# Linear attention, gated mixing and channel mixing on one core: the first block in float32 matmuls, the weights split in two only for the blocks behind it

## The chip, the cores and the metric

One core of a Trainium2 chip. The metric is the device time of one execution in microseconds (us). The engines are TensorE (PE; its weight loads are shown apart as PEld), VectorE (DVE), ScalarE (ACT), GpSimd (POOL) and SyncE (SP), which issues nearly all transfers.

## The reference

Three stages follow one another, all float32, with B=8, H=8, S=576, D=64, so 4608 rows of 512 values (weights and `conv_w` come as float64):

```python
q_s = softmax(q over d);  k_s = softmax(k over the sequence)
kv = einsum('bhsd,bhse->bhde', k_s, v);  x = einsum('bhsd,bhde->bhse', q_s, kv)   # x: 4608 x 512
gate = sigmoid(causal convolution of x, 5 taps, conv_w)
y = (gate * (x @ w_val)) @ w_out                                # 512x512 each
xk = mu_k*y + (1-mu_k)*y_prev;  xr = mu_r*y + (1-mu_r)*y_prev   # y_prev: one row earlier
out = sigmoid(xr @ w_r) * (relu(xk @ w_k)**2 @ w_v)             # 512x512, 512x1024, 1024x512
```

## The kernel before

The rows are cut into 12 blocks of T=384. Inside a block the 512 channels lie on partitions as 4 chunks of 128 and the 384 rows lie along the free axis. A block is a run of steps: V0 to V3 (x @ w_val, tile `pv`, one output chunk each), Y0 to Y3 (`py`), R0 to R3 (`racc`, one input chunk into three row tiles of 128x512), then H0 to H7 (`ph`) mixed with A0 to A7 (`vacc`, three row tiles, three steps behind H).

TensorE gets float32 accuracy from fp32r operands: each operand is a high part and a rest (`xh` and `xl`, `w_val_hi` and `w_val_lo`), and each product is three passes: high by high, high by rest, rest by high (L505 `products`, L559 for R, L591 for A, L448 for x). So a V, Y, H step is 12 passes of 384 columns for each output chunk, an R or A step 9 passes of 512.

Beside the steps stands the side work. Rounds (two for each batch, four heads each) make `kv`: `max` (DVE, tile `pm`), `turn` (transposes `pmT`, `mx`, exp of `kt`) and `mm` (`kvacc`). Then, for the next block, come `qload`, `qexp`, `qnorm` (softmax of q, tile `qt`), `xturn` (transposes `pq`), `x` (`px`) and `gate` (the convolution).

The weights arrive as 28 pieces of 128x512 float64 values, 512 KB each, in tiles `raw`. A piece is decoded to the negative of its float32 in place, by ACT (L148) and two DVE operations (L149, L150), and split at once: ACT writes the high part (L233), the rest comes from DVE (L235) for the names in `LOW_ON_VECTOR` and for the others from TensorE, an identity matmul of the decoded weight and one or two of the high part (tile `pl`, L241, L243) that ACT copies out (L244). Seven places hold such tiles: three in pool `first`, four in pool `early`.

In block 0 TensorE also computes the convolution of chunks 0, 2 and 3 (tile `pg`, L476, a diagonal matrix for each tap, built by ACT at L472), and ACT does the exp of q in 24 pieces of 128x64 (L385).

What stands where is written out by hand: `PROLOGUE` is all that comes ahead of V0, `FIRST` the side work behind each step of block 0, `REST` that of every later block. The building layer then places the instructions on the engines, and may move one past another there. An engine runs its instructions in order, and SP too: a load that waits for a place holds up those behind it. The order is the two queues' and the engines' own; there is no planner at run time.

Of the kernel before, what the change touches and what calls it, by code (L numbers as in the profile page):

```python
# [732 lines left out]
```

## Time and profile before

| | us |
|---|---|
| median of 3 runs (833.97, 835.52, 835.59) | 835.52 |
| the profiled execution | 834.17 |
| its span in the trace | 832.4 |
| TensorE busy in the span | 805.2 (97%) |
| VectorE busy | 565.8 (68%) |
| ScalarE busy | 505.6 (61%) |

The span starts with the first instruction that the trace shows, so the profiled execution is 1.77 us longer than its span. The first matmuls of V0 start at 47.09 us in block 0, at 127.90 in block 1 and at 192.90 in block 2. These three times cut the span into the stretches that the rows below use. A busy share is an average over the whole span: which engine ends a wait is read in each stretch.

### The profile page before, as it was taken

Reading aid. Unit: us, or ns where it says so; the run is one execution under the profiler, and the core shown is the slowest. Engines: PE = TensorE matmul, PEld = TensorE weight load, DVE = VectorE, ACT = ScalarE, POOL = GpSimd, SP = SyncE. Lnnn points to the kernel's source line nnn. Section 1 sums busy time; section 2 is a strip of 40 time slices with the busy share of each in tenths; the row PEclk is TensorE's granted clock in tenths of the full one; section 3 lists DMA queues with packets and bytes.
Section 4 is the critical chain, followed back from the end, with each engine's and each line's share of the span. In section 5 each row is a group of like instructions: output and inputs, shape, how many; then the busy total and the mean of one; then the engine's idle time right before and its main releaser. Section 6 shows DMA issues by size and latency. Waiting matters only on the chain.

```text
span 832.4 us, 12622 instructions
## 1 busy us (share of the span) xinstructions
PE 805.2 (97%) x4705; PEld 725.2 (87%) x4705; DVE 565.8 (68%) x1022; ACT 505.6 (61%) x1042; POOL 46.8 (6%) x208
## 2 busy tenths in 40 slices
PE   3699999999999999999999999999999999999998
PEld 2477888999989999999999999999998998998996
DVE  5799979677658578568576767757765866653621
ACT  5999674763763763763774674674674575564552
POOL 1001000100000100100000100100000000010000
PEclk9999999999999999999999999999999999999999
DMA  9688241211251211211232201202204101100101
GB/s 227 238 250 248 63 99 45 55 38 39 60 100 38 61 38 39 61 39 39 61 66 72 61 22 55 61 6 70 61 8 92 39 1 39 39 1 1 38 1 39
DMA packets 102124, 54.33 MB, mean 65 GB/s; under 512 B 85650, under 2 KB 93870, under 8 KB 102062
## 3 DMA queue, kind: packets, MB, share of 16 engines
q1 hardware_dynamic: 102016, 53.49, 24.9%
q8 instruction: 37, 0.61, 0.3%
q14 instruction: 25, 0.20, 0.1%
q10 hardware_dynamic: 46, 0.02, 0.0%
HBM read 44.06 MB, written 9.44 MB: 64 GB/s over the span
## 4 chain that ended last, share of the span: by engine, by line
PE 88%; DVE 4%; DMA 3%; ACT 2%; issue 1%; SPq 0%; DVEq 0%; ACTq 0%
PE vacc L591 23%; PE ph L505 23%; PE py L505 11%; PE pv L505 11%; PE racc L559 11%; PE px L448 3%; PE kvacc L327 3%; PE pq L433 2%; DMA raw<-in_moe_w_v_dram 1%; PE pg L476 1%; DMA raw<-in_moe_w_r_dram 1%; ACT qt L385 1%; DVE raw L150 1%; DMA raw<-in_moe_w_val_dram 1%; PE pl L241 1%
## 5 line engine op out<-in xcount | busy, mean ns | idle before, releaser
L505 PE MATMUL ph<-xkh,w_k_hi 128*128 128x384 f32 x384 | 132.5, 345 | 0.3 <-ACT yf L538 0.3
L505 PE MATMUL ph<-xkl,w_k_hi 128*128 128x384 f32 x384 | 129.2, 337 | 0.0
L505 PE MATMUL ph<-xkh,w_k_lo 128*128 128x384 f32 x384 | 129.1, 337 | 0.0
L406 DVE TENSOR_TENSOR kl<-rf,kh 128x384 fp32r<-128x384 f32 x96 | 53.4, 556 | 95.3 <-ACT kh L405 94.1
L591 PE MATMUL vacc<-w_v_hi,kl 128*128 128x512 f32 x288 | 112.7, 393 | 1.1 <-DVE kl L406 1.1
L591 PE MATMUL vacc<-w_v_hi,kh 128*128 128x512 f32 x288 | 113.4, 394 | 0.0
L591 PE MATMUL vacc<-w_v_lo,kh 128*128 128x512 f32 x288 | 112.7, 391 | 0.0
L495 DVE SCALAR_TENSOR_TENSOR gate<-xf,cw,gate 128x384 f32<-128x384 f32 x180 | 110.5, 616 | 2.9 <-ACT gate L493 0.2
L579 ACT ACTIVATE rf<-ph 128x384 f32<-128x384 f32 x96 | 47.0, 490 | 93.1 <-PE ph L505 92.6
L505 PEld LDWEIGHTS ph<-xkh,w_k_hi 128*128 128x128 f32 x384 | 72.2, 188 | 3.1 <-ACT yf L538 0.6
L548 DVE SCALAR_TENSOR_TENSOR xm<-yf,mus,xm 128x384 f32<-128x384 f32 x96 | 57.3, 616 | 25.6 <-ACT xm L547 25.1
L505 PEld LDWEIGHTS ph<-xkh,w_k_lo 128*128 128x128 f32 x384 | 72.4, 189 | 2.1
L505 PEld LDWEIGHTS ph<-xkl,w_k_hi 128*128 128x128 f32 x384 | 72.2, 188 | 0.4 <-DVE xkl L406 0.3
L591 PEld LDWEIGHTS vacc<-w_v_hi,kl 128*128 128x128 f32 x288 | 53.9, 188 | 13.1 <-DVE kl L406 1.7
L505 PE MATMUL pv<-xl,w_val_hi 128*128 128x384 f32 x192 | 65.1, 339 | 0.0
L505 PE MATMUL pv<-xh,w_val_hi 128*128 128x384 f32 x192 | 65.0, 338 | 0.0
L505 PE MATMUL py<-gh,w_out_hi 128*128 128x384 f32 x192 | 64.9, 345 | 0.0
L505 PE MATMUL pv<-xh,w_val_lo 128*128 128x384 f32 x192 | 64.8, 338 | 0.0
L505 PE MATMUL py<-gl,w_out_hi 128*128 128x384 f32 x192 | 63.3, 340 | 0.0
L505 PE MATMUL py<-gh,w_out_lo 128*128 128x384 f32 x192 | 63.1, 335 | 0.0
L591 PEld LDWEIGHTS vacc<-w_v_hi,kh 128*128 128x128 f32 x288 | 54.1, 188 | 8.9 <-ACT kh L405 0.3
L591 PEld LDWEIGHTS vacc<-w_v_lo,kh 128*128 128x128 f32 x288 | 54.1, 188 | 8.4
(132 smaller groups left out, 1665.9 us busy)
## 6 DMA issues: line engine op xcount, KB each, us to landing
out_dram<-rs SPq DMA_DIRECT2D x36, 256.0 KB, 2.0
kt<-in_k_dram SPq DMA_DIRECT2D x16, 512.0 KB, 4.7
vt<-in_v_dram SPq DMA_DIRECT2D x64, 128.0 KB, 3.8
qt<-in_q_dram SPq DMA_DIRECT2D x32, 256.0 KB, 4.2
raw<-in_moe_w_k_dram SPq DMA_DIRECT2D x8, 512.0 KB, 5.3
raw<-in_moe_w_v_dram SPq DMA_DIRECT2D x8, 512.0 KB, 4.4
kt<-in_k_dram SPq DMA_DIRECT2D x32, 64.0 KB, 4.2
raw<-in_moe_w_val_dram SPq DMA_DIRECT2D x4, 512.0 KB, 5.1
```

Source lines behind the costliest of these rows:

```text
L150: nc.vector.scalar_tensor_tensor(out=high, in0=high, scalar=3, in1=low, op0=ALU.logical_shift_left, op1=ALU.bitwise_or)
L241: nc.tensor.matmul(pl[:, 0:WC], lhsT=f32(ident), rhs=t, start=True, stop=False)
L327: nc.tensor.matmul(acc[e * D:(e + 1) * D, x * VW:(x + 1) * VW], lhsT=kt[:, 2 * x + e, s, :], rhs=st["v"][:, 2 * x + e, s, :], start=(s == ...
L406: nc.vector.tensor_sub(pair[1], a, f32(pair[0]))
L433: nc.tensor.transpose(pq[:, t * P:(t + 1) * P], qt[:, t, 2 * c:2 * c + 2, :].rearrange("p h d -> p (h d)"), f32(ident))
L448: nc.tensor.matmul(px[:, o:o + n], lhsT=kvs[b % 2][w][:, c, :], rhs=(qh, ql)[a][:, o:o + n], start=(m == 0), stop=(m == 2),)
L495: nc.vector.scalar_tensor_tensor(out=gx(gate), in0=xv[:, :, HALO - sh:HALO - sh + L], scalar=tap(c, HALO - sh), in1=gx(gate), op0=ALU.mult ...
L505: nc.tensor.matmul(po, lhsT=pairs_l[c][w], rhs=pairs_r[c][a], start=start and c == 0 and m == 0, stop=stop and c == n - 1 and m == 2,)
L548: nc.vector.scalar_tensor_tensor(out=gx(xf), in0=yv[:, :, 1:], scalar=mu[:, c:c + 1], in1=gx(xf), op0=ALU.mult, op1=ALU.add)
L559: nc.tensor.matmul(st["r"][t], lhsT=xr[a], rhs=W_r[w][:, c, :], start=(c == 0 and m == 0), stop=(c == NC - 1 and m == 2),)
L579: nc.scalar.activation(rf, ph[:, :T], AF.Relu)
L591: nc.tensor.matmul(st["v"][t], lhsT=kk[a], rhs=W_v[w][:, f, :], start=(f == 0 and m == 0), stop=(f == NF - 1 and m == 2),)
```

## The change

Block 0 is computed with plain float32 matmuls, one per product (the hardware takes two matmul instructions for it in the trace). Its operands are not split: `decode_weight` writes the float32 weight into a tile `whole`, without the sign change, and the splits (`swval0` and so on) are steps of their own, placed at the end of block 0 and in block 1, the high part on ACT, the rest (`lower`) on DVE for all 28. x of the blocks 0 and 1 is computed the same way from a float32 `kvf`. V and Y of block 0 go input chunk by input chunk into four PSUM banks (`row`), so V0 needs x chunk 0 and one weight piece only. No convolution is left on TensorE. q of block 0 comes with one transfer in packets of 768 bytes and v of the first two rounds in packets of 1 KB (tile `dense`, spread out by an ACT copy) where packets of 256 bytes were used, and the exp of q is one ACT instruction again, with DVE doing the subtraction. The raw tiles have six places on one side, which `dense` shares, and one place (pool `first`) for the seven pieces in `LEFT_WEIGHTS`. One list, `FRONT`, replaces `PROLOGUE` and `FIRST` and reaches over block 1. In block 1 and later the second and third pass of a product change places. `REST` stays for blocks 2 to 11.

```diff
-PROLOGUE = (
-    "lk0 lwval0 cload lv0 qload lwval1 lk1 lv1 lwval2 lwval3 lwout0 lwout1 lwout2 lwr0 lwr1 lwr2 lwr3 "
-    "lwk0 lwk1 lwk2 lwout3 lwk3 consts max0 wval0 turn0 mm0 max1 qexp wval1 turn1 mm1 qnorm wval2 xturn0 "
-    "x0 wval3 wout3 xturn1 x1 own0 xturn2 x2 xturn3 x3 wout0 wout1 wout2 own2 own1"
+FRONT = (
+    "lwout0 lk0 qload.0 lk1 max0 cload lv0 lv1 lwval0 lwval1 lwval2 lwval3 lwout1 lwr0 lwout2 lwout3 qexp.0 turn0 "
+    "lwr1 consts lwr2 vcopy0 wval3 qnorm.0 max1 mm0 vcopy1 turn1 xturn0.0 wval0 mm1 wval1 x0.0 wval2 lwr3 xturn1.0 "
+    "x1.0 gate0.0 xturn2.0 V0.0 gate1.0 xturn3.0 x2.0 V1.0 x3.0 V2.0 wout1 V3.0 gf0.0 wout0 gate3.0 gf1.0 gate2.0 "
+    "gf2.0 lwk0 lwk1 lwk2 lwk3 wout2 gf3.0 wout3 Y0.0 wr0 Y1.0 wr1 Y2.0 wr2 Y3.0 y0.0 wk1 y1.0 y2.0 y3.0 wr3 lwv1 "
+    "lwk4 mixk0.0 wk0 lwk5 lwk7 R0.0 R1.0 lwk6 mixk1.0 R2.0 mixk2.0 wk2 R3.0 mixk3.0 wk3 lwv3 lwv2 H0.0 lwv0 wv1 lwv4 "
+    "lwv5 H1.0 wv0 wk4 H2.0 wk5 rsig.0 A0.0 H3.0 wk6 A1.0 wk7 H4.0 wv2 max2 A2.0 H5.0 wv3 lwv6 lwv7 turn2 A3.0 H6.0 "
+    "mm2 max3 wv4 A4.0 wv7 wv6 H7.0 wv5 A5.0 turn3 qload.1 qexp.1 qnorm.1 xturn0.1 A6.0 swval3 x0.1 xturn1.1 x1.1 "
+    "swval0 A7.0 mm3 xturn2.1 gate0.1 x2.1 swval1 swval2 gate1.1 xturn3.1 x3.1 V0.1 gate2.1 V1.1 gate3.1 max4 V2.1 "
+    "turn4 swout1 swout0 V3.1 swout2 swout3 qload.2 kvsplit Y0.1 Y1.1 swr0 Y2.1 swr1 qexp.2 qnorm.2 swr2 Y3.1 swk1 "
+    "R0.1 mixk0.1 mixk1.1 R1.1 swr3 R2.1 mixk2.1 mixk3.1 swk0 R3.1 swk2 xturn0.2 swk3 swv1 H0.1 x0.2 xturn1.2 H1.1 "
+    "rsig.1 gate0.2 H2.1 swv0 swk4 swk5 A0.1 x1.2 xturn2.2 mm4 H3.1 swk6 swk7 A1.1 gate1.2 H4.1 swv2 x2.2 xturn3.2 "
+    "A2.1 swv3 H5.1 swv4 A3.1 H6.1 gate2.2 x3.2 swv7 swv6 A4.1 H7.1 swv5 A5.1 A6.1 A7.1 gate3.2"
 ).split()
-FIRST = {
-    1: "own3 wr1 wr0",
-    2: "wr2 wr3 wk0 wk1 wk2",
...
-    27: "gate3 gate2",
-}
...
+LEFT_GAP, RIGHT_GAP = 96, 224
-LOW_ON_VECTOR = "wval3 wout1 wout2 wout3 wr0 wr1 wr2 wk0 wk1 wk3 wk6 wk7 wv0 wv3 wv4 wv5 wv6 wv7".split()
-Q_ON_SCALAR = True
-CONV_ON_TENSOR = (0, 2, 3)
+CONV_ON_TENSOR = ()
-FIRST_WEIGHTS = "wval1 wval2 wval3 wout0 wout2 wr0 wr1 wr3 wk0 wk1 wk3".split()
+LEFT_WEIGHTS = "wval1 wout2 wr2 wr3 wk2 wk7 wv2".split()
...
-    def minus_float32(raw):
+    def decode(raw, out):
 
         low, high = raw[:, :, 0], raw[:, :, 1]
-        nc.scalar.activation(f32(high), f32(high), AF.Prelu, scale=-(2.0 ** -112), alpha=2.0 ** 32)
+        nc.scalar.activation(f32(high), f32(high), AF.Prelu, scale=2.0 ** -112, alpha=2.0 ** 32)
         nc.vector.tensor_scalar(out=low, in0=low, scalar1=29, scalar2=None, op0=ALU.logical_shift_right)
         nc.vector.scalar_tensor_tensor(
-            out=high, in0=high, scalar=3, in1=low, op0=ALU.logical_shift_left, op1=ALU.bitwise_or
+            out=out.bitcast(U32), in0=high, scalar=3, in1=low, op0=ALU.logical_shift_left, op1=ALU.bitwise_or
         )
-        return f32(high)
...
-        scale = 0.5 if pair is W_out or pair is W_v else 1.0
-        t = minus_float32(raws[name])
-        h, l = hi[:, kc, c0:c0 + WC], lo[:, kc, c0:c0 + WC]
-        nc.scalar.activation(h, t, AF.Copy, scale=-scale)
-        if name in LOW_ON_VECTOR:
-            nc.vector.scalar_tensor_tensor(
-                out=l, in0=t, scalar=-scale, in1=f32(h), op0=ALU.mult, op1=ALU.subtract
-            )
-        else:
-            pl = ps_acc.tile([P, 512], F32, tag="acc", name="pl")
-            n = int(1 / scale)
-            nc.tensor.matmul(pl[:, 0:WC], lhsT=f32(ident), rhs=t, start=True, stop=False)
-            for x in range(n):
-                nc.tensor.matmul(pl[:, 0:WC], lhsT=ident, rhs=h, start=False, stop=x == n - 1)
-            nc.scalar.activation(l, pl[:, 0:WC], AF.Copy, scale=-scale)
+    PLACES = len(CHUNKS) + 1
+    raws, whole, upper, lower = {}, {}, {}, {}
+
+    def place(dtype, name):
+        return wts.tile([P, WC], dtype, tag="w", bufs=PLACES, name=name)
+
+    def load_weight(n):
+        w, (kc, c0) = CHUNKS[n]
+        here = n in LEFT_WEIGHTS
+        raw = raws[n] = (first if here else early).tile([P, WC, 2], U32, tag="raw", bufs=1 if here else 6, name="raw")
+    def decode_weight(n):
+        w, at = CHUNKS[n]
+        whole[w, at] = place(F32, "whole")
+        decode(raws[n], whole[w, at])
...
+        h, t = upper[w][:, kc, c0:c0 + WC], whole[at]
+        l = lower[at] = place(F32R, "lower")
+        scale = 0.5 if w in HALF else 1.0
+        nc.scalar.activation(h, t, AF.Copy, scale=scale)
+        nc.vector.scalar_tensor_tensor(out=l, in0=t, scalar=scale, in1=f32(h), op0=ALU.mult, op1=ALU.subtract)
+
+    def weight(i, w, kc, c0, n):
+
+        at = w, (kc, c0 // WC * WC)
+        o = c0 % WC
+        if i == 0:
+            return (whole[at][:, o:o + n],)
+        return upper[w][:, kc, c0:c0 + n], lower[at][:, o:o + n]
...
+        if b == 0:
+            st["dense"] = early.tile([P, HR, NS4, D], F32, tag="raw", bufs=6, name="dense")
+            nc.sync.dma_start(
+                st["dense"].rearrange("p h s d -> p h (s d)"), src[:, 0:KT, :].rearrange("h (p s) d -> p h (s d)", s=NS4)
+            )
+    def v_copy(st):
+        nc.scalar.copy(st["v"][:, :, 0:NS4, 0:D], st["dense"])
...
+        if b < 2:
+            for e in range(2):
+                p = slice(e * D, (e + 1) * D)
+                nc.vector.tensor_mul(
+                    kvf[b][p, n * j:n * (j + 1), p], sums[p, :, 0:D], d3[p].to_broadcast([D, n, D])
+                )
+            return
...
+            came = first.tile([P, H, NT, D], F32, name="came")
+            nc.sync.dma_start(
+                came.rearrange("p h t d -> p h (t d)"), q[0, :, 0:T, :].rearrange("h (p t) d -> p h (t d)", t=NT)
+            )
+            return qt, came
...
-        for x in range(n):
-            nc.scalar.activation(a[:, x, :], a[:, x, :], AF.Exp, bias=qm[:, x:x + 1], accum_out=qs[:, x:x + 1])
...
-    PASSES = ((0, 0), (0, 1), (1, 0))
+    def passes(po, left, right, start, stop):
+
+        m = ((0, 0),) if len(left) == 1 else ((0, 0), (1, 0), (0, 1))
+        for x, (a, b) in enumerate(m):
+            nc.tensor.matmul(
+                po, lhsT=left[a], rhs=right[b], start=start and x == 0, stop=stop and x == len(m) - 1
+            )
...
+            kv = (kvf[b],) if i < 2 else kvs[b % 2]
+            passes(px[:, o:o + n], tuple(a[:, c, :] for a in kv), tuple(a[:, o:o + n] for a in st["q", c]), True, True)
...
+        def row(po, w, c, a):
+
+            for m in range(NC):
+                passes(po[m][:, :T], weight(i, w, c, m * P, P), a, c == 0, c == NC - 1)
...
+                row(st["pv"], "wval", m, xs["x", m])
+                row(st["py"], "wout", c, st["g", c])
...
+                passes(st["r"][t], part(st["xr", c], t), weight(i, "wr", c, 0, DM), c == 0, c == NC - 1)
...
+                    passes(st["v"][t], part(st["k", f], t), weight(i, "wv", f, 0, DM), f == 0, f == NF - 1)
```

SP, the first transfers, before (`kt`, `vt`, `qt` are k, v and q; `raw` a weight piece):

```order
L273 DMA kt<-in_k_dram 128x4x256
L278 DMA kt<-in_k_dram 64x4x64 x2
L221 DMA raw<-in_moe_w_val_dram 128x1024
L285 DMA vt<-in_v_dram 128x4x64 x4
L286 DMA vt<-in_v_dram 64x4x64
L362 DMA qt<-in_q_dram 128x8x64 x3
L221 DMA raw<-in_moe_w_val_dram 128x1024
L273 DMA kt_117<-in_k_dram 128x4x256
L278 DMA kt_117<-in_k_dram 64x4x64 x2
L285 DMA vt_118<-in_v_dram 128x4x64 x4
L286 DMA vt_118<-in_v_dram 64x4x64
L221 DMA raw<-in_moe_w_val_dram 128x1024 x2
```

and after:

```order
L205 DMA raw<-in_moe_w_out_dram 128x1024
L272 DMA kt<-in_k_dram 128x4x256
L277 DMA kt<-in_k_dram 64x4x64 x2
L382 DMA came<-in_q_dram 128x8x192
L272 DMA kt_115<-in_k_dram 128x4x256
L277 DMA kt_115<-in_k_dram 64x4x64 x2
L285 DMA dense<-in_v_dram 128x4x256
L291 DMA vt<-in_v_dram 64x4x64
L285 DMA dense<-in_v_dram 128x4x256
L291 DMA vt_116<-in_v_dram 64x4x64
L205 DMA raw<-in_moe_w_val_dram 128x1024 x4
L205 DMA raw<-in_moe_w_out_dram 128x1024
```

A piece of w_out comes first, the q of block 0 is one transfer instead of three, the v of a round is two instead of five, and all four pieces of w_val stand together behind them.

TensorE ahead of V0, before (`pq` are transposes of q, `px` makes x, `pg` the convolution, `pv` is V0):

```order
L433 MATMUL pq<-ident,qt 128x128 x3
L243 MATMUL pl<-w_out_hi,ident 128x512 x2
L448 MATMUL px<-qh,kv_hi_108 128x384
L448 MATMUL px<-qh,kv_lo_109 128x384
L476 MATMUL pg<-xf,diag 128x384
L448 MATMUL px<-ql,kv_hi_108 128x384
L476 MATMUL pg<-xf,diag 128x384 x4
L505 MATMUL pv<-xh,w_val_hi 128x384
```

and after:

```order
L335 MATMUL kvacc<-vt_116,kt_115 64x65 x20
L457 MATMUL pq<-ident,qt 128x128 x3
L430 MATMUL pv<-xf,whole 128x384
L430 MATMUL px<-q,kvf_108 128x384
L457 MATMUL pq<-ident,qt 128x128 x3
L430 MATMUL pv<-xf,whole 128x384 x3
L457 MATMUL pq<-ident,qt 128x128 x3
L430 MATMUL px<-q,kvf_108 128x384
```

V0 starts behind the first chunk of x instead of behind all four and the convolution, and the other chunks follow between its matmuls.

VectorE in block 1 around its Y and R steps, before (`gl`, `xrl`, `xkl` are rests of activations that PE waits for, `xm` the mixes, `pm` and `kt` a round, `qs` and `qt` q):

```order
L406 TENSOR_TENSOR gl<-gf,gh 128x384
L526 SCALAR_TENSOR_TENSOR gf<-gate,pv 128x384
L314 TENSOR_TENSOR kt<-kt,mx 128x1280
L406 TENSOR_TENSOR gl<-gf,gh 128x384
L393 TENSOR_REDUCE qs<-qt 128x24
L394 TENSOR_SCALAR qs<-qs 128x24
L548 SCALAR_TENSOR_TENSOR xm<-yf,mus,xm 128x384
L395 RECIPROCAL qs<-qs 128x24
L396 TENSOR_TENSOR qt<-qt,qs 128x1536
L406 TENSOR_TENSOR xrl<-xm,xrh 128x384
```

and after:

```order
L423 TENSOR_TENSOR gl<-gf,gh 128x384
L399 TENSOR_REDUCE qm<-qt 128x24
L322 TENSOR_TENSOR kt<-kt,mx 128x1280
L593 SCALAR_TENSOR_TENSOR xm<-yf,mus,xm 128x384 x2
L400 TENSOR_TENSOR qt<-qt,qm 128x1536
L423 TENSOR_TENSOR xrl<-xm,xrh 128x384
L593 SCALAR_TENSOR_TENSOR xm<-yf,mus,xm 128x384
L423 TENSOR_TENSOR xrl<-xm,xrh 128x384
L231 SCALAR_TENSOR_TENSOR lower<-whole,wk_hi 128x512 x2
L423 TENSOR_TENSOR xrl<-xm,xrh 128x384
L407 TENSOR_REDUCE qs<-qt 128x24
L593 SCALAR_TENSOR_TENSOR xm<-yf,mus,xm 128x384
```

Two weight splits (`lower`) stand between the `xrl` of R1 and R2 now, and the maximum, the subtraction and the sum of the next q (`qm`, `qt`, `qs`) stand in the same run, where only the sum and the division stood.

## Rows read from the trace of the kernel before

**Rows 1.** Windows: four stretches; busy us (instructions) per engine, clock, DMA share, GB/s.

```profile
0.00:47.09 47.09, 26.71 (x147) 16.45 (x148) 32.52 (x67) 36.85 (x111) 6.04 (x32) 1.00 0.84 233
47.09:127.90 80.81, 79.07 (x456) 65.90 (x455) 71.11 (x130) 63.21 (x124) 5.08 (x20) 1.00 0.55 154
127.90:192.90 65.00, 63.79 (x370) 58.31 (x369) 49.39 (x87) 39.18 (x77) 4.41 (x13) 1.00 0.18 45
192.90:832.40 639.50, 635.60 (x3737) 584.53 (x3735) 412.79 (x741) 366.40 (x732) 31.22 (x143) 1.00 0.18 44
```

**Rows 2.** Waits of PE, 47.09 to 832.4: us in total, times, longest.

```profile
PE pmT L301 <- DVE pm L294: 1.2, 1, 1.2
```

**Rows 3.** Chain that ended last, 0 to 60: start us, us, what.

```profile
2.99 4.86 DMA raw<-in_moe_w_val_dram
...
9.86 2.08 PE pl L241 x2
...
20.82 4.69 ACT qt L385 x28
...
33.69 6.23 DMA raw<-in_moe_w_r_dram
...
44.97 2.58 PE pg L476 x8
...
57.19 0.90 PE pl L241 x2
```

**Rows 4.** Windows by 10 us, columns as in rows 1.

```profile
0.00:10.00 10.00, 0.54 (x3) 0.44 (x3) 4.50 (x11) 3.94 (x11) 3.79 (x25) 1.00 0.77 193
10.00:20.00 10.00, 6.55 (x48) 4.21 (x49) 5.36 (x10) 7.01 (x22) 0.00 (x0) 1.00 1.24 255
20.00:30.00 10.00, 4.47 (x25) 1.87 (x25) 7.00 (x14) 9.78 (x45) 0.00 (x0) 1.00 0.50 175
30.00:40.00 10.00, 9.03 (x55) 6.00 (x52) 9.00 (x22) 9.08 (x21) 1.24 (x5) 1.00 0.86 290
```

**Rows 5.** Waits of SP's queue, 0 to 130: us in total, times, longest.

```profile
SPq L221 <- PE pl L241: 13.1, 6, 4.1
```

**Rows 6.** Chain, 700 to 795: three-pass products of a late block.

```profile
708.50 8.35 PE pv L505 x48
...
778.43 8.47 PE py L505 x48
786.90 8.20 PE racc L559 x36
```

**Rows 7.** Windows for tile pl alone, block 0: PE, PEld, ACT busy.

```profile
47.09:127.90 80.81, 8.58 (x20) 3.55 (x20) 3.59 (x6) 1.00 0.55 154
```

**Rows 8.** The same for tile pg.

```profile
47.09:127.90 80.81, 4.12 (x12) 1.79 (x10) 1.01 (x2) 1.00 0.55 154
```

**Rows 9.** Chain, 128 to 195: a round's matmuls and one chunk's q transposes.

```profile
142.61 1.32 PE kvacc L327 x40
...
158.57 0.33 PE pq L433 x3
```

**Rows 10.** VectorE groups, 47.09 to 127.9: busy us, mean ns, idle before.

```profile
L150 DVE SCALAR_TENSOR_TENSOR raw<-raw 128x512 uint32<-128x512 uint32 x17 | 11.7, 690 | 0.3 <-ACT raw L148 0.2
L495 DVE SCALAR_TENSOR_TENSOR gate<-xf,cw,gate 128x384 f32<-128x384 f32 x12 | 7.4, 617 | 0.5 <-ACT gate L493 0.2
L149 DVE TENSOR_SCALAR raw<-raw 128x512 uint32<-128x512 uint32 x16 | 6.7, 427 | 0.9 <-DMA raw<-in_moe_w_v_dram 0.9
...
L235 DVE SCALAR_TENSOR_TENSOR w_v_lo<-raw,w_v_hi 128x512 fp32r<-128x512 f32 x6 | 4.2, 693 | 0.3 <-ACT w_v_hi L233 0.2
L373 DVE TENSOR_TENSOR qt<-qt,qm 128x1536 f32<-128x1536 f32 x2 | 3.5, 1756 | 0.0
```

**Rows 11.** ScalarE groups, same stretch and columns.

```profile
L148 ACT ACTIVATE raw<-raw 128x512 f32<-128x512 f32 x17 | 11.5, 683 | 2.2 <-DMA raw<-in_moe_w_v_dram 1.7 <-DMA raw<-in_moe_w_k_dram 0.4
...
L233 ACT ACTIVATE w_v_hi<-raw 128x512 fp32r<-128x512 f32 x8 | 5.3, 667 | 0.0
```

More of the change, by code (lines that the diff above doesn't have):

```diff
@@ L188, in tap @@
         return cw[:, t * NC + c:t * NC + c + 1]
-    def gap(pool, size, name):
-        pool.tile([P, size // 4], F32, name=f"gap_{name}")
-    def weight(name, rows, cols, pool=wts):
-        hi = pool.tile([P, rows // P, cols], F32R, name=f"{name}_hi")
-        lo = pool.tile([P, rows // P, cols], F32R, name=f"{name}_lo")
-        return hi, lo
-    W_val = weight("w_val", DM, DM)
-    gap(wts, 64, "out")
-    W_out = weight("w_out", DM, DM)
-    gap(wts, 128, "k")
-    W_k = weight("w_k", DM, DFF)
@@ new lines, in tile_linear_attention_gated_conv_channel_mix @@
+    HALF = ("wout", "wv")
+    SHAPES = {"wval": (w_val, DM, DM), "wout": (w_out, DM, DM), "wr": (w_r, DM, DM), "wk": (w_k, DM, DFF), "wv": (w_v, DFF, DM)}
+    CHUNKS = {
+        f"{w}{x}": (w, at) for w, (_, rows, width) in SHAPES.items()
+        for x, at in enumerate((kc, c0) for c0 in range(0, width, WC) for kc in range(rows // P))
+    }
+    PLACES = len(CHUNKS) + 1
+    raws, whole, upper, lower = {}, {}, {}, {}
+    def place(dtype, name):
+        return wts.tile([P, WC], dtype, tag="w", bufs=PLACES, name=name)
@@ L499, in x_gate @@
         nc.scalar.activation(gate, gate, AF.Tanh, scale=0.5)
-    def products(po, pairs_l, pairs_r, start, stop):
-        n = len(pairs_l)
-        for c in range(n):
-            for m, (a, w) in enumerate(PASSES):
-                nc.tensor.matmul(
-                    po, lhsT=pairs_l[c][w], rhs=pairs_r[c][a],
-                    start=start and c == 0 and m == 0, stop=stop and c == n - 1 and m == 2,
-                )
-    def cols(pair, kc, c0, n):
-        return tuple(t[:, kc, c0:c0 + n] for t in pair)
     def main_steps(i, xs):
@@ L550, in mix, with part @@
             )
[L551 removed]
+            st[key, c] = (xf,) if i == 0 else split(xf, pair(key))
+        def part(pair, t):
+            return tuple(a[:, t * P:(t + 1) * P] for a in pair)
         def r(c):
             if c == 0:
[L555 removed]
+                st["r"] = [bank(ps_acc, "acc", f"racc{t}") for t in range(NT)]
             for t in range(NT):
[L557 to L562 removed]
+                passes(st["r"][t], part(st["xr", c], t), weight(i, "wr", c, 0, DM), c == 0, c == NC - 1)
         def rsig():
@@ L676, in tile_linear_attention_gated_conv_channel_mix @@
-    own = {f"own{c}": lambda c=c, st=xs: x_gate(st, 0, c) for c in range(NC)}
-    pro.update(own)
-    pro.update(weight_parts("wval", w_val, W_val, DM, DM))
-    pro.update(weight_parts("wout", w_out, W_out, DM, DM))
-    wide = weight_parts("wr", w_r, W_r, DM, DM)
-    wide.update(weight_parts("wk", w_k, W_k, DM, DFF))
-    wide.update(weight_parts("wv", w_v, W_v, DFF, DM))
-    pro.update(wide)
-    with tc.issue_after(cast.ins):
-        for n in PROLOGUE:
-            pro[n]()
-    for i in range(NB):
-        steps, side = main_steps(i, xs)
-        side.update(rounds_of(take_rounds((1, 1, 2)[i % 3] if i else NR)))
-        xs = {}
-        if i + 1 < NB:
-            side.update(attention(i + 1, xs))
-        if i == 0:
-            side.update(wide)
-            side.update(own)
-        for x, f in enumerate(steps):
+        todo_front[f"lk{x}"] = lambda x=x: k_load(rounds[x])
@@ L697, in tile_linear_attention_gated_conv_channel_mix @@
+    with tc.issue_after(cast.ins):
+        for n in FRONT:
+            todo_front.pop(n)()
+            if n == START:
+                break
+    for n in FRONT[FRONT.index(START) + 1:]:
+        todo_front.pop(n)()
+    for i in range(2, NB):
+        steps, side = main_steps(i, acts[i])
+        side.update(rounds_of(new_rounds(i)))
+        if i + 1 < NB:
+            side.update(attention(i + 1, acts[i + 1]))
+        for x, f in enumerate(steps.values()):
             f()
-            for n in (REST if i else FIRST).get(x, "").split():
+            for n in REST.get(x, "").split():
```

274 lines of the change are left out of this document (136 added, 138 removed).

## The prediction

> **What bounds the kernel now.** I read the windows by stage first [rows 1], then PE's waits, then the chain that ended last. From the first matmul of V0 on (47.09 us) PE is busy 79.07 of 80.81 us in block 0, 63.79 of 65.00 in block 1 and 635.60 of 639.50 in the ten blocks behind. Its longest wait there is 1.2 us, once [rows 2]. So from 47.09 on the time is PE's own work, and DVE (71.11 us in block 0) and ACT (63.21) run beside it. Ahead of 47.09 PE is busy 26.71 us only, and the chain there [rows 3] goes through loads of 4.86 and 6.23 us, a run of 4.69 us of the exp pieces on ACT, and 2.58 us of the convolution on PE. The transfers move 193, 255, 175 and 290 GB/s in the four stretches of 10 us [rows 4]. Time can therefore be won in two places: the 47 us ahead of V0, and PE's work in block 0. The ten late blocks keep their work.
>
> **Prices.** A fp32r pass of 384 columns is 8.35/48 = 0.174 us, one of 512 columns 8.20/36 = 0.228 [rows 6], so three passes are 0.522 and 0.683. A float32 product of 384 columns is two instructions; eight of the convolution's take 2.58 us [rows 3], so one product is 0.645. For 512 columns the nearest row is the identity matmul of a weight, 0.90 for the pair at 57.19 [rows 3], reading every second word; by columns of the convolution's row it would be 0.86. I take 0.88. A float32 product thus costs more than three passes here, 0.645 against 0.522: the change adds PE work where it replaces products, and must win by what it takes away and by starting earlier.
>
> The Trainium skill ("FP8 and Floating Point Precision", section "TensorE Precision Notes") says that true float32 takes four passes through the array. Four passes by the rows would be 0.696 and 0.911, and with them the sum below would be 4.4 us longer; the convolution's row shows less, and the row decides.
>
> **The change, part by part.**
>
> *Start of V0, 47.09 to 29.* V0 now needs one chunk of x and one piece of w_val. The exp of q becomes one instruction, the convolution's matmuls and diagonal matrices go, and no weight is split. Loads then end last. Ahead of V0 stand in SP's order: a piece of w_out 0.52 MB, k of two rounds 1.31, q 0.79, v of two rounds 1.18, four pieces of w_val 2.10. A second piece of w_out, 0.52, counts too, because DVE does its shift ahead of the last decode step of w_val and runs in order. Together 6.42 MB. The kernel before has moved 1.93 + 2.55 = 4.48 MB by 20 us [rows 4]; the other 1.94 at 255 to 290 GB/s end at 26.7 to 27.6. Behind them come one shift (0.43) and two decode steps of 0.69 [rows 10]: 28.5 to 29.4. I take 29, that is -18.1. The lower end, without the second w_out piece, is 27. The upper end, the 193 GB/s of the first stretch throughout, is 33.3 + 1.8 = 35.1.
>
> *Block 0 on PE, 80.8 to 85.4.* From V0 to the V0 of block 1:
> - V: 16 products at 0.645 = 10.3; three chunks of x behind its start 1.9 and two sets of q transposes at 0.33 [rows 9] 0.7: 12.9.
> - Two products at double price at the start, 1.3. In the trace a float32 pair took 2.08 at 9.86 us and 0.90 at 57.19 [rows 3], and V0 now lies between.
> - Y 10.3; R 12 at 0.88 = 10.6; H 32 at 0.645 = 20.6; A 24 at 0.88 = 21.1.
> - Two kv rounds: 1.32 [rows 9] and four transposes at 0.11, together 3.5; one wait of PE such as the row shows, 1.2 [rows 2].
> - x of block 1, four times 0.33 + 0.645 = 3.9.
>
> Together 85.4, which is +4.6. As a check: the products alone rise from 58.0 to 73.0, while the identity matmuls of the splits (8.58 [rows 7]) and the convolution (4.12 [rows 8]) leave the stretch, and three chunks of x come into it. DVE takes over the convolution of all chunks, 16 steps of 0.62 [rows 10] in block 0, ahead of Y; PE's V hides them, with some 2 us to spare by my count of DVE's row (11 gate steps, 4 decode steps and 3 shifts ahead of the first `gf`, 10.9 us, end it at 41 where Y0 starts at 43). Without that cover Y0 waits for the difference.
>
> *Block 1, 65.0 to 66.2.* The splits that stood in block 0 come here for w_k and w_v: 16 times 0.69 on DVE [rows 10] and 0.67 on ACT [rows 11]. With them DVE has 49.4 + 11.0 = 60.4 us in 65, ACT 49.9. So it fits, and PE's work hides it, but two splits stand directly ahead of the rest that R2 needs, and the subtraction of the next q (1.76 [rows 10]) in the same run. I charge 1.2, the size of the one wait in the trace [rows 2]; the ends are 0 and 4 (all of the run's splits and the subtraction late once).
>
> *Nothing for:* the other order of passes in blocks 1 to 11. The rows hold 0.174 for V and 8.47/48 = 0.176 for Y [rows 6]; that spread, 2 ns over some 1900 passes of a kind, is 4 us either way at most, and I take 0. The ACT copies of v, 2 pieces, lie beside loads. The first piece of w_out ahead of k costs 2 us of the start and is in the 6.42 MB.
>
> The sum against the profiled execution: 834.17 - 18.1 + 4.6 + 1.2 = 821.9. The median of the runs is 1.35 above that execution, so 823.
>
> **Rivals.**
>
> *Weights come late.* Seven pieces share one place: each is loaded (4.86 to 6.23 us [rows 3]), decoded (0.68 on ACT, 0.43 and 0.69 on DVE), and only then the next can start, and SP holds back all loads behind one that waits; six such waits took 13.1 us in the kernel before [rows 5]. Block 0 on PE is now the consumer from 29 us on. By my count H0 has some 3 us to spare on the fifth piece of that chain (w_k) and A0 about as much on its first w_v piece. If each of five steps takes 2 us more than the load and the decode alone, because the decode stands behind gates in DVE's row, PE waits 10 - 3 = 7 us: 830. A start by the upper end, 35.1, gives 829. For it: the serial chain and the queue order. Against: the loads behind it have six places, and moved 290 GB/s between 30 and 40.
>
> *Better start.* V0 at 27, no double price, no wait in block 1: 823 - 2 - 1.3 - 1.2 - 1.2 = 817.
>
> *TensorE stays at the price of the start, slower than before.* The early pair cost 2.08 where the later cost 0.90 [rows 3], and PE was busy 6.55 and 4.47 of 10 us from 10 to 30 [rows 4]; the granted clock column reads 1.00 in all stretches. If the matmuls of V, Y and R, 31.2 us, all ran at double price, the time would be 823 + 31 = 854. It decides from 12.5 us of float32 work at double price, some 19 products. Against it: PE has hardly a gap from V0 on, and the pair at 57.19, in a stretch without gaps, is at the low price.
>
> The Trainium skill ("TensorE: Matmul & The Clock Gate", "Part 1: The HAM clock gate") says that the array's clock is halved when the engine has been idle and comes back with work. By it V0 after the waiting of the start would begin at the low clock; the 2.08 against 0.90 agrees with that in size, while the clock column does not show it.
>
> *V0 does not move.* If a load that I have not counted holds x or w_val until 42 us or later, -5 of start against +4.6 + 1.2 leaves the time within 0.2%. Nothing in the rows asks for it: q, k and w_val are all issued ahead.
>
> **How the numbers follow.** The forecast, 818 to 828, has 0.63; late weights or start, 829 to 833, 0.18; the better start 0.09; the slow price 0.06; no movement 0.04. The first three are faster, together 0.90. The range of 815 to 832 holds the forecast, the better start for the most part and most of the late case, some 0.82. About 0.2% (1.7 us) is what a measurement of this kernel can tell from no change. Faster by more than that 0.90, within it 0.04, slower 0.06.
>
> **What would show it.** In the changed profile: the first `pv` at 29 (27 to 33 is right, above 35 the start was mis-sized); V, Y and H products 0.645 apart in the chain and R and A 0.86 to 0.90; the V0 of block 1 at 114 and of block 2 at 181; the ten late blocks 639.5 us within 2. Late weights would show as PE waiting on `whole` in R, H or A of block 0, and in the chain as loads into `raw`. The slow price would show as products 1.2 us and more apart with PE full. Block 1 over 69 us with PE waiting for `xrl` or `kl` would mean that the splits on DVE have become the bound there. The prediction is wrong if PE works with gaps between 29 and 114.

## The result

The changed kernel takes 825.15 us (median of 4 runs, 823.94 to 826.32), the kernel before 834.75 (4 runs, 833.85 to 835.59): a ratio of 0.9885, 95% interval 0.9864 to 0.9906, so 1.15% faster. The profiled execution took 824.69 us, its span 822.9, and the cuts by V0 give this table:

| stretch | before [rows 1] | predicted | after |
|---|---|---|---|
| up to V0 of block 0 | 47.09 | 29 | 27.21 |
| block 0 | 80.81 | 85.4 | 86.07 |
| block 1 | 65.00 | 66.2 | 66.91 |
| blocks 2 to 11 | 639.50 | 639.5 | 642.71 |
| span | 832.4 | 820.1 | 822.9 |

One sentence ahead of the prediction is too wide: the second and third pass of a product change places in R and A alone. V, Y, H and x keep their order.

The windows of the changed kernel, cut at its own V0 starts (the columns are those of [rows 1]):

```profile
0.00:27.21 27.21, 11.15 (x99) 7.74 (x99) 18.85 (x37) 12.70 (x19) 4.72 (x28) 1.00 0.85 287
27.21:113.28 86.07, 83.99 (x329) 46.50 (x329) 68.42 (x128) 51.52 (x96) 7.69 (x20) 1.00 0.55 169
113.28:180.19 66.91, 64.98 (x370) 58.63 (x370) 65.16 (x111) 50.52 (x102) 6.20 (x19) 1.00 0.25 59
180.19:822.90 642.71, 638.49 (x3737) 585.57 (x3735) 410.47 (x737) 365.88 (x731) 30.98 (x142) 1.00 0.16 44
```

TensorE is still busy nearly throughout. It starts its blocks 19.9 us earlier, pays 5.3 us more in block 0 and 1.9 more in block 1, and, what was not forecast, 3.2 more in the ten late blocks, whose work is the same. In block 1 VectorE is busy 65.16 of 66.91 us, where it was 49.39 of 65.00.

The chain that ended last up to V0 (start us, us, what):

```profile
3.07 5.76 DMA came<-in_q_dram
...
10.94 1.67 DVE qt L400
...
13.74 1.48 DVE kt L322
15.21 1.66 DVE qs L407
...
17.99 1.76 DVE qt L410
...
21.10 0.91 PE pq L457 x3
...
22.56 1.65 PE px L430 x2
24.21 2.37 PE kvacc L335 x40
26.58 0.83 PE pq L457 x3
27.41 1.00 PE pv L430 x2
28.41 0.65 PE px L430 x2
```

One transfer, that of q, then VectorE's work on q and k nearly without a gap from 10.9 to 20 us, then TensorE. No load of a weight stands in it. The last five rows show a price that falls: a product of 384 columns (`px`, two instructions) costs 1.65 us at 22.56 and 0.65 at 28.41.

What TensorE waited for from 27 to 113 us, and from 113 to 190 (us in total, times, longest):

```profile
PE racc L430 <- DVE xm L593: 1.0, 1, 1.0
PE px L430 <- ACT q L463: 0.6, 1, 0.6
PE kvacc L335 <- ACT kt L325: 0.5, 1, 0.5
```

```profile
PE py L430 <- DVE gf L566: 1.8, 1, 1.8
```

Three short waits in block 0, none of them for a weight by this view, and one of 1.8 us in the first Y step of block 1. The wait of 1.0 us, for a mix (`xm`), goes back to a weight all the same. In the chain that ended last, ahead of it:

```profile
42.27 7.42 DMA raw<-in_moe_w_k_dram
...
49.70 0.71 ACT raw L141
50.41 0.38 ACT yf L584
```

A piece of w_k lands, ACT decodes it, and only then comes the copy of y (`yf`) from which the mix is made.

### The profile page after: what moved, and what is told of

Same layout as the page of the kernel before. It is cut to its first block, busy times and chain, and to the rows that moved or that the text cites. A ratio compares the mean times of both kernels' runs of the same rounds, so it can differ in the third digit from the quotient of the medians.

```text
span 822.9 us, 12129 instructions
## 1 busy us (share of the span) xinstructions
PE 798.6 (97%) x4530; PEld 698.4 (85%) x4530; DVE 562.9 (68%) x1010; ACT 480.6 (58%) x947; POOL 49.6 (6%) x208
## 4 chain that ended last, share of the span: by engine, by line
PE 89%; DVE 5%; DMA 2%; ACT 2%; issue 1%; SPq 0%; DVEq 0%; ACTq 0%
PE vacc L430 24%; PE ph L430 23%; PE pv L430 11%; PE py L430 11%; PE racc L430 11%; PE px L430 4%; PE kvacc L335 3%; PE pq L457 2%; DVE whole L143 1%; DMA raw<-in_moe_w_k_dram 1%; DMA raw<-in_moe_w_v_dram 1%; DVE gate L525 1%; DMA came<-in_q_dram 1%; DVE xm L593 0%; DVE qt L400 0%
## 5 line engine op out<-in xcount | busy, mean ns | idle before, releaser
L430 PE MATMUL ph<-xkh,wk_hi 128*128 128x384 f32 x352 | 121.2, 344 | 0.0
L430 PE MATMUL ph<-xkl,wk_hi 128*128 128x384 f32 x352 | 118.7, 337 | 0.0
L430 PE MATMUL ph<-xkh,lower 128*128 128x384 f32 x352 | 118.3, 336 | 0.0
L430 PE MATMUL vacc<-lower,kh 128*128 128x512 f32 x264 | 104.1, 394 | 0.0
L430 PE MATMUL vacc<-wv_hi,kl 128*128 128x512 f32 x264 | 103.9, 394 | 0.0
L430 PE MATMUL vacc<-wv_hi,kh 128*128 128x512 f32 x264 | 103.8, 394 | 0.0
L430 PEld LDWEIGHTS ph<-xkh,wk_hi 128*128 128x128 f32 x352 | 66.2, 188 | 2.3
L430 PEld LDWEIGHTS ph<-xkh,lower 128*128 128x128 f32 x352 | 66.2, 188 | 2.0
L430 PEld LDWEIGHTS ph<-xkl,wk_hi 128*128 128x128 f32 x352 | 66.0, 188 | 0.0
L430 PE MATMUL py<-gh,wout_hi 128*128 128x384 f32 x176 | 59.8, 346 | 1.8 <-DVE gf L566 1.8
```

The source lines that it names most:

```text
L430: nc.tensor.matmul(po, lhsT=left[a], rhs=right[b], start=start and x == 0, stop=stop and x == len(m) - 1)
```

## Experiments

Experiments 1 to 11 are one run each, so they are read by their stages and waits and not by their total. Two stages differ from run to run even where nothing in them was changed: in the changed kernel and the seven runs with the same start and block 0 (e1, e2, e5, e8, e9, e11, e12), V0 comes between 26.8 and 28.2 us and block 0 takes 84.8 to 86.4.

### The late blocks: four runs on the pace

Rows of the late blocks, before (chain, start us, us, what):

```profile
735.93 2.08 PE ph L505 x12
...
745.95 2.06 PE vacc L591 x9
```

and after:

```profile
749.12 2.08 PE vacc L430 x9
751.21 2.10 PE ph L430 x12
...
776.87 8.20 PE racc L430 x36
```

One H step is 0.02 us longer and one A step too; R takes 8.20 for 36, as in [rows 6]. Eighty steps of each kind come to about 3 us, which is the difference. The table has the time of the chain's pieces over their matmuls, from the V0 of block 2 on (the expectations below have H and A of the changed kernel 0.1 lower):

| kernel | H, ns | A, ns | R, ns | late blocks, us |
|---|---|---|---|---|
| before | 174.5 | 229.4 | 227.8 | 639.5 |
| changed | 175.9 | 231.2 | 227.8 | 642.7 |
| e1_shift | 175.6 | 232.9 | 227.9 | 643.5 |
| e2_order | 175.9 | 231.2 | 227.8 | 642.7 |
| e8_gap | 175.9 | 231.3 | 227.8 | 642.8 |
| e9_kvgap | 175.9 | 231.1 | 233.2 | 644.1 |

**e1_shift**, 96 bytes ahead of two high parts:

```diff
+        if side == "left":
+            pool.tile([P, 24], F32, name="upper_gap")
```

> The changed kernel with 96 bytes of padding ahead of the high parts of w_k and w_v, nothing else. The ten late blocks take 642.5 us in the changed kernel (from the V0 of block 2 on) and 639.5 in the kernel before; H passes are 175.8 ns apart against 174.5, A passes 231.1 against 229.4. Theory place: where operands lie against each other sets the pace, so H and A move by a nanosecond or more per pass and the late blocks by 2 us or more, most likely back to 640. Rival order: the pace hangs on the order of the passes in R and A, and the padding changes nothing (642.5 within 0.5).

A moved by 1.6 ns, the wrong way; the mean of H moved by 0.2. The late blocks took 643.5 us.

**e2_order**, the old pass order in R and A:

```diff
+                passes(st["r"][t], part(st["xr", c], t), weight(i, "wr", c, 0, DM), c == 0, c == NC - 1, ((0, 1), (1, 0)))
...
+                    passes(st["v"][t], part(st["k", f], t), weight(i, "wv", f, 0, DM), f == 0, f == NF - 1, ((0, 1), (1, 0)))
```

> The changed kernel with the pass order of the kernel before in R and A (the rest of the weight second, the rest of the activation third); places are untouched. Theory place: H stays at 175.8 ns, A at 231, R at 227.8, the late blocks at 642.5 within 0.5. Rival order: A goes back to 229.4 ns, the late blocks to about 641; H cannot be explained by it.

Nothing moved: the order of the passes is not the cause.

**e8_gap**, all of the left side 256 bytes further:

```diff
-LEFT_GAP, RIGHT_GAP = 96, 224
+LEFT_GAP, RIGHT_GAP = 352, 224
```

> The changed kernel with 256 more bytes of padding in front of all that stands on the left side (weights' rests, kv, activations, w_k and w_v high parts move together; w_val, w_out and w_r high parts stay). Theory place: H, A or Y change their pace by 1 ns per pass or more against 175.8, 231.1 and 178.8. Rival relative: only the place of operands against each other counts, so H and A stay at 175.8 and 231.1 within 0.2.

Nothing moved, although the left side shifted against w_val, w_out and w_r on the right.

**e9_kvgap**, 64 bytes between the rests of the weights and what follows:

```diff
+    kvp.tile([P, 16], F32, name="kv_gap")
```

> The changed kernel with 64 bytes of padding between the places of the weights' rests and all that stands behind them on the left (kv, activations, the high parts of w_k and w_v). Moving everything on the left by 256 bytes left H at 175.8 and A at 231.1 ns; moving the high parts alone by 96 moved A to 232.8. Theory relative place: the rests now lie differently against activations and high parts, so H (one chunk of which costs 7 to 10 ns more per pass than the others) or A changes by 1 ns per pass or more. Rival: neither changes by more than 0.3 ns, and the place of the rests has no part in it.

H and A kept their pace, against the theory's expectation for them, but R lost 5.3 ns per pass. Its row in the chain:

```profile
716.35 8.39 PE racc L431 x36
```

So where operands lie against each other changes the pace of R and A (e9, e1), and the whole side's place and the pass order do not (e8, e2). One run each is enough for that: the pace of A agrees within 0.1 ns in the nine traces of the changed kernel, e2 to e4, e7, e8 and e10 to e12. The 1.8 ns by which A is slower than before are of the size that a shift makes; which neighbours make it was not found, and no run brought A back to 229.4.

For H the mean stayed within 0.3 ns in all these runs, but its slow passes moved. By the start times of the late H steps, on average, the passes of the second input chunk are 182, 175 and 180 ns apart and those of the third and fourth 173; in the kernel before all four chunks are at 173 to 174. With the gap of e1 the three are 177, 175 and 174 and the later ones up to 176; with that of e9 they are 175, 175 and 181. So place has a part in H too. Why its mean stays 1.2 to 1.4 ns above that of the kernel before is open.

### The start: packets and the price of TensorE's work

**e3_packets** takes the long packets away again:

```diff
-        if b == 0:
+        if False:
             st["dense"] = early.tile([P, HR, NS4, D], F32, tag="raw", bufs=6, name="dense")
...
-        if i == 0:
+        if False:
             came = first.tile([P, H, NT, D], F32, name="came")
```

> The changed kernel with q of block 0 and v of the first two rounds loaded in packets of 256 bytes, as in the kernel before; the ACT copies of v go with it. Theory packets: the 270 and 379 GB/s of the first 20 us come from the longer packets, so they fall to about 200 and 255 and the first V0 starts at 29 to 33 instead of 27.2. Rival chain: V0 is ended by the work of DVE on q and by PE's products, and starts at 27 to 28 as before, whatever the transfers do.

V0 started at 33.06 us, and the transfers moved 222 and 238 GB/s in the first two stretches of 10 us instead of 270 and 379. That is the upper end of what the theory of packets gave. TensorE now waits for a decoded piece of w_val just ahead of V0, as it does not in the changed kernel:

```profile
PE pv L431 <- DVE whole L143: 2.6, 1, 2.6
```

SP's timeline shows why that piece is late, with the short packets (start us, us, instruction):

```profile
3.62 3.27 SPq L391 DMA_DIRECT2D qt<-in_q_dram  x3
...
9.09 2.72 SPq L290 DMA_DIRECT2D vt<-in_v_dram  x4
...
15.89 2.07 SPq L205 DMA_DIRECT2D raw<-in_moe_w_val_dram  x4
```

and with the long ones, in the changed kernel:

```profile
3.07 0.61 SPq L382 DMA_DIRECT2D came<-in_q_dram  x1
...
6.85 0.61 SPq L285 DMA_DIRECT2D dense<-in_v_dram  x1
...
11.02 2.03 SPq L205 DMA_DIRECT2D raw<-in_moe_w_val_dram  x4
```

Each issue costs SP 0.3 to 1.6 us, and not by its bytes: one of 512 KB of a weight 0.33 to 0.68, one of 64 KB of v 0.59. Three transfers of q took 3.27 us of SP and one takes 0.61; four of v took 2.72 and one takes 0.61. So the first piece of w_val is issued at 11.0 instead of 15.9. The weights land later behind their issue, too: by the landings that the two traces have up to 30 us, w_val takes 7.2 us at the median (6.4 in the changed kernel), w_out 8.0 (4.0). The run changes the length of the packets and the number of issues together, so what each of them costs alone is not shown.

**e4_warm** puts 14 unread products ahead of TensorE's first work (`heat10` ahead of the first transposes, `heat4` ahead of the first round):

```diff
+            tc.keep_in_program_order(
+                nc.tensor.matmul(hot["t"][:, 0:P], lhsT=f32(ident), rhs=f32(ident), start=True, stop=True)
+            )
```

> The changed kernel with 14 products of 128x128 on TensorE that nobody reads, ten ahead of the first transposes and four ahead of the first round's matmuls. In the changed kernel 40 matmuls of the first round take 2.43 us at 16.6 us (1.39 later) and the first chunk of x 1.65 (0.65 later). Theory idle: TensorE runs at the high price because it stood idle before; with work ahead the round takes 1.4 to 1.9 us, the first chunk of x about 0.65, and V0 starts 1 to 3 us earlier. Rival place or operands: the prices stay at 2.43 and 1.65 and V0 stays at 27.2 or is later by the added products.

**e6_warm2** fills the gaps between its steps too, with 35 products. The same steps put products into later rounds as well (84 such matmuls in the chain behind 183 us), so its time, 841.47 us, is not to be compared and only its first 30 us count.

```diff
+    HOT = {"max0": 14, "consts": 6, "mm0": 4, "xturn0.0": 2}
...
+            heat(HOT.get(n, 0))
```

> The changed kernel with 35 unread products of 128x128 on TensorE, put into the gaps between its own steps from 5 to 22 us so that it hardly stands idle. With 14 products (the run before) the first stretch was cheaper by 0.8 us: the transposes fell from 0.69 to 0.44, the first round stayed at 2.44. Theory idle: with the gaps filled both rounds take 1.4 to 1.6 us, the first chunk of x 0.8 to 0.9 (two instructions and their latency), and V0 starts at 24.5 to 25.5. Rival: weights or the work of DVE end V0 anyway, the prices fall and V0 stays at 26 to 26.5. Rival place: prices stay, V0 at 27 or later.

The first round and the first chunk of x in the timeline (start us, us, instruction), changed kernel:

```profile
16.62 2.43 PE L335 MATMUL kvacc<-vt,kt 128*64 128x65 f32 x40 [2.10 <-issue]
...
22.56 1.65 PE L430 MATMUL px<-q,kvf 128*128 128x384 f32 x2 [0.57 <-ACT q L465]
```

e4_warm:

```profile
16.57 2.44 PE L335 MATMUL kvacc<-vt,kt 128*64 128x65 f32 x40
...
22.16 1.50 PE L430 MATMUL px<-q,kvf 128*128 128x384 f32 x2 [0.57 <-ACT q L465]
```

e6_warm2:

```profile
18.46 1.43 PE L335 MATMUL kvacc<-vt,kt 128*64 128x65 f32 x40 [0.48 <-issue]
...
23.27 0.91 PE L430 MATMUL px<-q,kvf 128*128 128x384 f32 x2
```

With the gaps filled the round costs 1.43 instead of 2.43 us and the product 0.91 with its latency: TensorE is at its high price because it stands idle in between. But V0 comes at 26.79 (26.45 in e4), 0.4 to 0.8 us earlier, which is no more than it varies without any such change. The theory of idleness holds for the prices. The rival holds for V0 in so far as cheap matmuls do not bring it to 25.5; that the work of DVE and ACT would end it at about 26 us anyway is not shown, since in e6 the added products themselves stand in the chain ahead of the second round, with 1.09 and 0.67 us.

### Block 0: cover and slack

**e7_conv** gives the convolution of three chunks back to TensorE:

```diff
-CONV_ON_TENSOR = ()
+CONV_ON_TENSOR = (0, 2, 3)
```

> The changed kernel with the convolution of chunks 0, 2 and 3 of block 0 on TensorE again, the diagonals on ACT. Theory cover: PE's V hides the 12 steps of DVE that this takes away, so nothing comes back, PE has 30 more matmuls at 0.323 = 9.7 us, and V0 of block 1 comes 9 to 10 us later than in the changed kernel. Rival: DVE is late for Y0 and for the mixes in block 0 (it is in the chain from 36 to 42 us and from 53 to 59), so shedding 7.4 us of DVE gives back 2 us or more and the loss is under 8.

Block 0 took 99.99 us instead of 86.07, a loss of 13.9, more than TensorE's own 9.7 and outside both expectations. The changed kernel has no wait for a gate in Y0 that fewer steps on DVE could end, so the cover holds; and a cost shows that neither theory had: R waits for a mix three times as long as in the changed kernel, and Y waits too:

```profile
PE racc L430 <- DVE xm L593: 3.1, 1, 3.1
PE py L430 <- ACT gate L521: 1.0, 1, 1.0
```

The diagonals are not what makes ACT late, for the last of them is done at 28.9 us. Ahead of R it stands still for a load of a weight, with the copy of y behind it:

```profile
63.10 0.68 ACT L141 ACTIVATE raw<-raw 128x512 f32<-128x512 f32 x1 [2.19 <-DMA raw<-in_moe_w_k_dram]
63.68 0.48 ACT L584 ACTIVATE yf<-py 128x384 f32<-128x384 f32 x1
```

This is the path of late weights, by ACT's order and not by a wait of TensorE's own. TensorE stands idle 2.5 us longer than in the changed kernel. It is also busy 11.4 us longer, 9.7 of them with the convolution; the rest goes with the granted clock, which is 0.50 from 65.4 to 68.8 us, behind the long wait.

**e10_raw5** has five raw places on the right instead of six:

```diff
-        raw = raws[n] = (first if here else early).tile([P, WC, 2], U32, tag="raw", bufs=1 if here else 6, name="raw")
+        raw = raws[n] = (first if here else early).tile([P, WC, 2], U32, tag="raw", bufs=1 if here else 5, name="raw")
```

> The changed kernel with five places for raw weights on the right instead of six, so that loads start later and wait more for decoded pieces. Theory slack: in the changed kernel PE waits for no weight in block 0 (its one long wait there is 1.0 us for a mix), so there is slack of a few us and block 0 stays within 1 us of 86.1. Rival weights: the weights arrive just in time, and with one place less PE waits for decoded pieces in R, H or A and block 0 takes 89 us or more.

Block 0 took 87.62 us, between the two expectations, with a wait for a weight that the changed kernel does not have:

```profile
PE vacc L430 <- DVE whole L143: 1.4, 1, 1.4
```

With six places TensorE itself waits for no weight, and with five it does. The slack is there, and one place is about its size; block 0 ends up 1.2 us above the highest of the runs that do not change it, so the wait is the better witness.

### Block 1: what fills VectorE

**e5_gates** moves the maximum and turn of kv round 4 and the split of kv behind Y0, and holds two rests on DVE (of kv and of one piece of w_k) and twelve high parts of w_k and w_v on ACT to the order in which the program names them:

```diff
+    "swout1 swout0 V3.1 swout2 swout3 qload.2 Y0.1 max4 turn4 kvsplit Y1.1 swr0 swr3 Y2.1 swr1 qexp.2 qnorm.2 swr2 Y3.1 swk1 "
...
+        if w == "wv" or n in ("wk4", "wk5", "wk6", "wk7"):
+            tc.keep_in_program_order(hi)
+        if n == "wk1":
+            tc.keep_in_program_order(lo)
```

> The changed kernel with another order in block 1 alone: the maximum and turn of kv round 4, the split of kv and two weight splits leave the stretch ahead of Y0 (they follow Y0), and seven high parts of w_k and w_v wait for their turn on ACT. In the changed kernel PE waits 1.8 us in Y0 for the third gf, and in three of five traces the granted clock falls to 0.90 over 113 to 130 us behind it and block 1 takes 68.4 to 68.7 us instead of 66.9. Theory queue: the wait is DVE's row of gates with other work between them, so it shrinks to under 0.6 us, the clock does not fall and block 1 takes 65.0 to 65.8. Rival total: DVE has too much to do in block 1 (65 of 67 us busy), so the wait only moves to R or H and block 1 stays at 66.5 or more.

The wait in Y0 was gone and the clock stayed at 1.00, but TensorE waited 3.4 us elsewhere from 113 to 182 us:

```profile
PE ph L434 <- DVE lower L231: 1.6, 1, 1.6
PE racc L434 <- DVE xrl L427: 0.9, 1, 0.9
PE pmT L313 <- DVE pm L306: 0.5, 1, 0.5
PE ph L434 <- ACT wk_hi L230: 0.4, 1, 0.4
```

From the V0 of block 1 to the end it took 712.2 us against 709.6.

**e11_light** is the same without holding back the high parts of w_k and w_v, with the split of kv one step later and the rest of a piece of w_r held to its place too.

> The changed kernel with kv round 4 and the split of kv behind Y0 of block 1 and two splits of weights kept in the order in which the program names them; the high parts of the weights are free to run when ACT has time (two runs before, where seven of them were held back too, PE waited 1.6 us in H0 for a rest and 2.1 us in R, and the wait in Y0 was gone). Theory queue: without the held-back high parts H0 does not wait, and blocks 1 together with the late ones take 707.5 to 708.5 us instead of 709.6. Rival total: DVE is full from 113 to 150 us (19.7 of 20 us in the changed kernel), and what leaves Y0 is missing in R or H: 709.5 or more.

H0 did not wait, R waited 1.7 us, and blocks 1 and later took 710.6: the rival again.

**e12_pool** gives three subtractions to GpSimd:

```diff
+        if n in ("wk1", "wr3"):
+            tc.keep_in_program_order(nc.gpsimd.tensor_sub(l, t, f32(h)))
...
+        tc.keep_in_program_order(nc.gpsimd.tensor_sub(lo, kvf[1], f32(hi)))
```

> The changed kernel with three subtractions of block 1 (the rest of kv, of one piece of w_k and of one of w_r) on GpSimd instead of VectorE, behind GpSimd's own small copies. They take 0.69 us each on DVE and stand between the gates ahead of Y0, where PE waits 1.8 us for the third gf; moving work behind Y0 only moved the wait to R and H, because DVE is full until 150 us. Theory full DVE: 2.0 us less on DVE there shrink the wait in Y0 by 1 to 1.8 us and it does not come back in R or H: block 1 takes 65.2 to 66.0 us instead of 66.9 and the whole time is 0.1 to 0.3% under the changed kernel's. Rival: GpSimd's work slows DVE or comes late itself (PE waits for a rest in R3 or H0), and block 1 is at 66.9 or more.

It was slower than the changed kernel: 827.66 us (6 runs), a ratio to the kernel before of 0.9922 (0.9908 to 0.9936) against 0.9885. Block 1 took 71.41 us, with 4.0 us of waits and a granted clock of 0.91 over 130 to 150 us. One row each of GpSimd and DVE shows a first reason:

```profile
114.68 1.68 POOL L367 TENSOR_TENSOR kv_lo<-kvf,kv_hi 128x512 fp32r<-128x512 f32 x1
```

```profile
115.12 1.65 DVE L528 SCALAR_TENSOR_TENSOR gate<-xf,cw,gate 128x384 f32<-128x384 f32 x1
```

The gate step beside the subtraction took 1.65 us where the others take 0.61. The same happens beside the other two subtractions: a mix takes 1.65 instead of 0.61, a small step on `qs` 1.25 instead of 0.17. DVE loses 3.2 us by this and is spared three subtractions of 0.69, 2.1 us. So none of the three versions of block 1 beats the changed kernel.

The waits of block 1 also have a second price. The same wait of 1.8 us stands in nine of the traces (the changed kernel, e1 to e4 and e7 to e10). In four of them the granted clock falls behind it (0.86 over 121 to 133 us in e1, e2 and e4, 0.91 over 130 to 150 in e7, whose block 1 starts later), and block 1 takes 68.4 to 68.7 us; in the other five it stays at 1.00 and block 1 at 66.8 to 67.0. What decides between the two is not shown. Windows behind the wait in e1_shift and in the changed kernel:

```profile
126.00:130.00 4.00, 4.00 (x17) 3.81 (x17) 3.88 (x7) 2.24 (x6) 0.00 (x0) 0.58 0.01 2
```

```profile
122.00:130.00 8.00, 6.17 (x38) 5.77 (x37) 8.00 (x15) 7.65 (x16) 0.56 (x3) 1.00 0.00 1
```

So a short wait costs 1.8 us in some executions and some 3.4 in others. The runs of the changed kernel lie 2.4 us apart, and the longest of them (826.32) has the lowest mean clock, 0.994.

## Why the prediction was right, and where it was not

The forecast was 823 (818 to 828) and the time is 825.15. Sign and size are right, and the terms of block 0 are; the start and block 1 came out near their forecasts by other paths than the prediction's, which is in part luck. Step by step, by the spans:

- **Start, 29 forecast, 27.21.** Right in size, wrong in mechanism. The working let loads end V0 at the 255 to 290 GB/s of [rows 4]. The changed kernel moves 270 and 379 GB/s in the first 20 us, and the chain goes by q, DVE and TensorE. e3 shows that the working's rates belong to short packets and many issues: with these V0 comes at 33, inside the bounds given, and TensorE waits 2.6 us for a decoded piece of w_val, the path that the working had. The longer packets and fewer issues were worth 5.9 us of the start, and the prediction gave them no price of their own. How the other 14 us of the earlier start divide among the exp, the convolution, the splits and the wait for all of x, no run shows.
- **Block 0, 85.4 forecast, 86.07.** The terms hold: H costs 2.58 for eight instructions, 0.645 each product, as the convolution's row in [rows 3] said, and 512 columns cost 0.86, the lower of the two ends. The chain, in block 0:

```profile
96.04 2.58 PE ph L430 x8
98.62 2.58 PE vacc L430 x6
```

The rule of four passes in the Trainium skill ("FP8 and Floating Point Precision", "TensorE Precision Notes") would be 0.696 and 0.911 by the rows of passes; the trace has 3.7 and 3.8 of them. The waits of block 0 came to 2.1 us where 1.2 was charged.

- **Block 1, 66.2 forecast, 66.91.** The size is right, the place is not. The charge was for splits ahead of R2; the trace has none there, and 1.8 us in Y0, for a `gf` (the gated rows that Y multiplies) behind gates, kv maxima and two splits. The count of 60.4 us for DVE was too low by 4.8 (65.16): it added the 16 splits of w_k and w_v alone. Beside them the changed kernel has 26 gate steps in block 1 where there were 21 (0.61 each), two maxima and two subtractions of q where there was one of each (1.75 each), the split of kv and one of w_r (0.69 each), one rest of x more (0.56), and two output steps less (0.68 each). These durations make 7 us and busy time rises by 4.8 only, because steps that follow one another overlap in the trace. In e5 and e11 DVE is busy 19.1 and 19.8 of the 20 us from 130 to 150, so a reordering only moves the wait.
- **Late blocks, +0 forecast, +3.2.** The failed step, and the whole miss of the span (822.9 against 820.1, made of -1.8, +0.7, +0.7 and +3.2). The prediction put the pace "for nothing" with 4 us either way at most, gave pass order as the only reason for a change, and named 639.5 us within 2 as a sign; the late blocks took 642.7. H 1.4 ns over 960 passes, A 1.8 over 720, Y 0.6 over 480 make 3.0 us. The order is not the cause (e2). Place is the likely one and is not shown to be it: a shift of 96 bytes moves A by 1.6 (e1) and the slow passes of H as well, but no run brought the old pace of H or A back.
- **Rivals.** The weights were late only in part. Of the two signs that the prediction names, TensorE waiting on `whole` is absent, but loads into `raw` do stand in the chain of block 0 (7.42 us of w_k at 42.27, 6.86 of w_v at 60.31), and the first of them is behind the wait of 1.0 us in R. e10 and e7 show how near more was: one place less costs 1.4 us of waiting for a piece, and with the convolution on TensorE R waits 3.1 us behind a load. The better start came true as to V0 alone, 1.8 us, and the late blocks lost more than that. The price of the start stayed with TensorE only to about 28 us. By the Trainium skill ("TensorE: Matmul & The Clock Gate", "Part 1: The HAM clock gate") an idle array runs at half its clock until it has worked for a while; e6 agrees, where the round fell from 2.43 to 1.43 when the gaps before it were filled.

## What to carry to other kernels

A product in full float32 costs 3.7 of the cheap passes, not three, and still wins here in a kernel's first block when it takes the splits, and with them the wait for all weights, off the start. Where the first loads decide, count SP's issues and not only bytes: one transfer of q in place of three and two of v in place of five, with longer packets, moved V0 by 5.9 us here. Where an engine works in order, ask what a load that it waits for holds up behind it: a wait that the profile names for a mix was one for a weight. And when buffers move, read the pace of the steps that did not change: 1 to 2 ns per pass over thousands of passes is a term of the sum.
